# Chunked attention and a Mish feed-forward: the scores of the third group of heads follow the values directly, and sums of w_out's units 5 to 7 move

## The chip, the core and the metric

One core of a Trainium2 chip runs the whole program. The metric is the device time of one execution in microseconds (us). Engines: PE (TensorE, matmuls), PEld (its weight loads), DVE (VectorE), ACT (ScalarE), POOL (GpSimd), SP (the engine on whose queue nearly all transfers are issued).

## What is computed

The reference, cut down: attention inside chunks of 64 tokens, then a feed-forward layer with Mish, all in float32.

```python
scores = scale * np.matmul(q_c, k_c.transpose(0, 1, 2, 4, 3))
scores = scores - np.max(scores, axis=-1, keepdims=True)
attn = np.exp(scores)
attn = attn / (np.sum(attn, axis=-1, keepdims=True) + 1e-09)
out = np.matmul(attn, v_c)
...
h = x @ w_in
sp = np.where(h > 20.0, h, np.log1p(np.exp(np.minimum(h, 20.0))))
g = h * np.tanh(sp)
return (g @ w_out).astype(np.float32)
```

x is the attention's output, 4608 tokens of 512 values; w_in is 512 x 2048, w_out 2048 x 512.

## The kernel before

**Blocks.** The tokens are cut into 18 pairs of 256. A first block does pairs 0 and 1; then blocks m = 1 to 4 do four pairs each. While block m multiplies, the attention of the four pairs of block m + 1 is done beside it, so m = 4 has none. Every float32 operand is split into a rounded upper part and a rest, and a product is three sets of matmuls. Both layers use Strassen-like seven-product schemes, so sums of weight quarters are needed as operands: they are made on the chip once, stored to device memory, and loaded again as `w`/`late` tiles by `load_op` (line 831), nine products ahead of their use.

**Blocks m = 2 to 4** (BOTH_FROM = 2, line 797) have an upward half, `up_two(m, n)` for n = 0 to 3 (line 1087), and a downward half, `down_all(m)`. One `up_two` works on two units of w_in, i = 0 and 1, and runs the seven products k = 0 to 6 for each of them in turn. A product is six matmuls of 128x512. After product k of unit i the program calls `beside(h)` with h = 2k + i, so h counts 0 to 13, and all other work is hung on h. The engines take their instructions strictly in the written order (`manual_schedule`).

**Evictions in up_two** (lines 1150 to 1182). PSUM banks x (two of tag h), y and v (o0 to o3, given out by `flip`) hold the sums. x is copied by ACT after k = 0, 2 and 4 (G11, G21, G22; lines 1155, 1160, 1162) and read by Mish after k = 5 (G12). y is added by DVE to G11 after k = 1. v is added to G22 after k = 4 and to G21 after k = 6 (line 862). Mish activations (line 540) follow each. So the next product into a bank waits until that bank has been read.

**Attention beside it.** Pair j = first_pair(m + 1) + n belongs to n. Steps: `a_scores` (64x64 matmuls, line 298), `a_max` (324), `a_sub` (336), `a_exp` (345, ACT, with its own activation table, so that a table load stands before exp and before the next Mish), `a_inverse` (391 to 393), `a_norm` (398), `a_transpose` (409), `a_copy` (419, ACT), `a_values` (298), `a_raw` (430). From block GROUP_FROM on, the scores of pair j + 1 are done at h = 12 right behind the values of pair j, by `scores_apart` into the two y banks (line 359), with `max_apart` (370) at h = 12 and `sub_apart` (381) at h = 13; exp, inverse and normalisation then stand at h = 0, 2 and 3 of the next n. Before the change this holds for m = 3 alone; in m = 2 each n has its own scores at h = 1, and the steps at h = 1 to 7.

**Sums of w_out.** Unit u = 0 to 7 of w_out needs four steps: `t_whole` (line 237, DVE, adds upper part and rest), `t_sums` (246, DVE, three subtractions), `t_hi` (250, ACT cast to the upper part), `t_lo` (254, DVE, the rest) with the store of 1 MB to device memory on SP's queue (257). Units 4 to 7 are done in the upward half of m = 2 by the plan BUILDS_UP (line 888), which gives each step a place (n, h). Their tile is

```python
bld["o", u] = c_p.tile([P, 4, 2, 256], F32, name=f"t_{u}", tag="c")
```

and pool c_p has one buffer. In `beside` the order within one h is: S sums (`s_sums`: sums of two activated tiles of an earlier unit, lines 1078 and 1082), then the plan's steps, then attention. S sums in m = 2 stand at h = 5 and 9 of n = 1 to 3, two units' worth per n.

Of the kernel before, what the change touches and what calls it, by code (L numbers as in the profile page):

```python
# [24 lines left out]
def kernel(  # L25
# [244 lines left out]
    def load_qk(j, qk=None, ts=(BOTH,), queues=(nc.sync, nc.sync), pool=(at, "A")):  # L270
        if qk is None:
            if pool[0] is xo_p:
                both = xo_p.tile([P, 2, 2, H, CHUNK], F32, name=f"qk_{j}", tag="x")
                qk = [both[:, 0], both[:, 1]]
            else:
                qk = [
                    pool[0].tile([P, 2, H, CHUNK], F32, name=f"{n}_{j}", tag=pool[1]) for n in "qk"
                ]
        for t in ts:
            for x, src, queue in zip(qk, (q, k), queues):  # L280
                queue.dma_start(
                    out=x[:, t], in_=src[2 * j : 2 * j + 2][t].rearrange("t p h c -> p t h c")
                )
        st[j] = {"q": qk[0], "k": qk[1]}

    def load_v(j, vs=None):
        if vs is None:
            vs = at.tile([P, 2, H, D], F32, name=f"v_{j}", tag="A")
        nc.sync.dma_start(out=vs, in_=v[2 * j : 2 * j + 2].rearrange("t p h c -> p t h c"))
        st[j]["v"] = vs  # L290
# [23 lines left out]
    def a_scores(j, t=BOTH, place=HOME):  # L314
        small_mm(banks(j, "s", t, place), st[j]["q"], st[j]["k"], t)
# [7 lines left out]
    def a_max(j, t=BOTH):  # L323
        nc.vector.tensor_reduce(
            out=small(j, "m", t),
            in_=st[j]["s", t.start].rearrange("p c t g k -> p c (t g) k"),
            op=ALU.max,
            axis=AX.X,
        )

    def a_sub(j, t=BOTH):
        d = st[j]
        if t.start == 0:
            d["p"] = at.tile([P, 2, NG, 2, CHUNK], F32, name=f"p_{j}", tag="A")
        m = d["m", t.start]
        nc.vector.tensor_tensor(
            out=d["p"][:, t].rearrange("p t g c k -> p c (t g) k"),
            in0=d["s", t.start].rearrange("p c t g k -> p c (t g) k"),
            in1=m.unsqueeze(3).broadcast_to([P, 2, m.shape[2], CHUNK]),
            op=ALU.subtract,  # L340
        )

    def a_exp(j, t=BOTH):
        p = st[j]["p"][:, t]
        nc.scalar.activation(out=p, in_=p, func=AF.Exp, scale=SCALE)
# [42 lines left out]
    def a_inverse(j, t=BOTH):  # L388
        p = st[j]["p"][:, t].rearrange("p t g c k -> p (t g) c k")
        r = small(j, "r", t)  # L390
        nc.vector.tensor_reduce(out=r.rearrange("p c n -> p n c"), in_=p, op=ALU.add, axis=AX.X)
        nc.vector.tensor_scalar(out=r, in0=r, scalar1=1e-9, scalar2=None, op0=ALU.add)
        nc.vector.reciprocal(out=r, in_=r)

    def a_norm(j, t=BOTH):
        p = st[j]["p"][:, t].rearrange("p t g c k -> p c (t g) k")
        r = st[j]["r", t.start]
        nc.vector.tensor_tensor(
            out=p, in0=p, in1=r.unsqueeze(3).broadcast_to([P, 2, r.shape[2], CHUNK]), op=ALU.mult
        )  # L400
# [14 lines left out]
    def a_copy(j, t=BOTH):  # L415
        d = st[j]
        if t.start == 0:
            d["ps"] = at.tile([P, 2, H, CHUNK], F32, name=f"ps_{j}", tag="A")
        nc.scalar.copy(
            out=d["ps"][:, t].rearrange("p t h k -> p (t h k)"),  # L420
            in_=d["pt", t.start][:, : t.stop - t.start].rearrange("p t g n -> p (t g n)"),
        )
# [39 lines left out]
    def first_pair(m):  # L462
        return PAIRS + 4 * (m - 1)
# [159 lines left out]
    def run(plan_, key):  # L623
        for step, arg in plan_.get(key, ()):
            step(arg)
# [169 lines left out]

    LOOK, MORE = 5, 4
    BOTH_FROM = 2
    GROUP_FROM = BOTH_FROM + 1
    PRODUCTS = (
        ("A11", "B11"),  # L800
        ("A12", "B21"),
# [74 lines left out]
    def t_plan(*begins):  # L876
        plan_ = {}
        for n, places in begins:
            for step, place in zip(T_STEPS, places):
                plan_.setdefault(place, []).append((step, n))  # L880
        return plan_
# [4 lines left out]
    for n in range(NU):  # L886
        BUILDS_DOWN.setdefault(n + 1, []).append((t_keep, n))
    BUILDS_UP = t_plan(
        (4, [(0, h) for h in (4, 5, 6, 10)]),
        (5, [(0, 13), (1, 0), (1, 1), (1, 4)]),  # L890
        (6, [(1, h) for h in (10, 11, 12, 13)]),
        (7, [(2, h) for h in (4, 10, 12, 13)]),
    )

    def unit(m, u):
# [178 lines left out]
    def flip(m):  # L1074
        return OPEN if (m - BOTH_FROM) % 2 == 0 else (OPEN[0], OPEN[2], OPEN[1])
# [8 lines left out]
    def s_sums(u):  # L1084
        s_one(u)
        s_three(u)

    def up_two(m, n):
        units = (2 * n, 2 * n + 1)
        xt, yt, vt = flip(m)  # L1090
        j = first_pair(m + 1) + n
        on = m < QUADS
        x, y, v_ = {}, {}, {}

        def beside(h):
            at_ = (5, 9) if m == BOTH_FROM else (1, 2)
            if h in at_ and n:
                s_sums(2 * n - 2 + at_.index(h))
            if m == BOTH_FROM:
                run(BUILDS_UP, (n, h))  # L1100
            if h in (10, 11) and n == NU // 2 - 1:
                ready.append(operand(0, h - 10))
            if not on:
                return


            ahead = n and m >= GROUP_FROM
            if h == 1:
                if not ahead:
                    a_scores(j)  # L1110
                if m >= GROUP_FROM and not n:
                    load_qk(j + 1, pool=(ob_p, "ob"))
                load_v(j)
            if h == 2 and not ahead:
                a_max(j)
            if h == 3:
                if not ahead:
                    a_sub(j)
                if n < 3 and (n or m < GROUP_FROM):
                    load_qk(j + 1, pool=(ob_p, "ob"))  # L1120
            if h == (0 if ahead else 4):
                a_exp(j)
            if h == (2 if ahead else 6):
                a_inverse(j)
            if h == (3 if ahead else 7):
                a_norm(j)
            if h == 10:
                a_transpose(j)
                a_copy(j)
            if h == 12 and n < 3:  # L1130
                a_values(j)
                if m < GROUP_FROM:
                    a_raw(j)
                else:
                    scores_apart(j + 1, yt)
                    a_raw(j)
                    max_apart(j + 1)
            if h == 13 and n < 3 and m >= GROUP_FROM:
                sub_apart(j + 1)

        for k in range(7):
            for i, u in enumerate(units):
                if k == 0:
                    x[u] = bank(f"x_{m}_{u}", xt[i])
                    for name in GS:
                        z_new(u, name)
                if k == 1:
                    y[u] = bank(f"y_{m}_{u}", yt[i])
                if k == 3:
                    v_[u] = bank(f"v_{m}_{u}", vt[i])  # L1150
                o = y[u] if k == 1 else v_[u] if k in (3, 6) else x[u]
                product(k, o, k in (0, 1, 3))
                z = {name: G[u, name] for name in ("G11", "G12", "G21", "G22")}
                if k == 0:
                    nc.scalar.copy(out=z["G11"], in_=o)
                elif k == 1:
                    add(o, z["G11"])
                    mish(z["G11"], z["G11"])
                elif k == 2:
                    nc.scalar.copy(out=z["G21"], in_=o)  # L1160
                elif k == 4:
                    nc.scalar.copy(out=z["G22"], in_=o)  # L1162
                    add(v_[u], z["G22"])
                    if i:
                        for u_ in units:
                            mish(G[u_, "G22"], G[u_, "G22"])
                elif k == 5:
                    mish(z["G12"], o)
                elif k == 6:
                    add(o, z["G21"])  # L1170
                    mish(z["G21"], z["G21"])
                beside(2 * k + i)

    ready = []
# [5 lines left out]
    def operand(k, u):  # L1180
        d = {}
        g = G[u, TYPES[k][0]]
        d["gh"] = part("gh", f"gh_{k}_{u}")
        nc.scalar.copy(out=d["gh"], in_=g)  # L1184
        d["gl"] = part("gl", f"gl_{k}_{u}")
        parts["n"] += 1
        nc.vector.tensor_tensor(out=d["gl"], in0=g, in1=d["gh"].bitcast(F32), op=ALU.subtract)  # L1187
        return d
# [239 lines left out]
```

## Time and profile before

| | us |
|---|---|
| median of 3 runs (lowest to highest) | 806.84 (806.28 to 808.19) |
| the profiled execution's own time | 804.22 |
| its span, first to last instruction | 802.4 |
| PE busy | 787.6 (98%) |
| PEld busy | 680.7 (85%) |
| DVE busy | 547.5 (68%) |
| ACT busy | 462.6 (58%) |
| mean DMA traffic | 244 GB/s |

An engine's busy time is the time in which one of its instructions runs. PE's matmuls are pipelined and their ends are modelled, so PE's 98% does not mean that it is at its peak. The chain of waits follows the work that ended last back to the beginning; a piece of it ends when the next begins. In a list of instructions in order of time, the bracket at the end of a line tells how long the engine had been idle before it and what released it.

### The profile page before, as it was taken

What the parts mean: (1) busy time and instruction counts of PE and PEld (TensorE: products, weight loads), DVE (VectorE), ACT (ScalarE), POOL (GpSimd) and SP (SyncE); (2) the same over time, 40 slices, a digit from 0 to 9 for tenths busy, and PEclk for the clock granted to TensorE, in tenths of its full rate; (3) what the DMA queues carried; (4) which work ended last, traced back from release to release, by engine and by line L of the source; (5) the groups of instructions that cost most, each with busy time, mean ns of one, the idle gap of its engine ahead of it and who ended that gap; (6) DMA issues with size and microseconds to landing.
All of it is one profiled execution on the core that took longest, in us unless ns stands there. A gap on an engine that the chain in (4) does not pass through costs nothing.

```text
span 802.4 us, 16472 instructions
## 1 busy us (share of the span) xinstructions
PE 787.6 (98%) x6394; PEld 680.7 (85%) x6394; DVE 547.5 (68%) x835; ACT 462.6 (58%) x694; POOL 0.7 (0%) x6
## 2 busy tenths in 40 slices
PE   4999999999999999999999999999999999999998
PEld 4888787788888888888999998888999988888887
DVE  6789898655656786676688945545698723338875
ACT  5998976534436445566655737566556434455443
POOL 0000000000000000000000000000000000000000
PEclk9999999999999999999999999999999999999999
DMA  9999989877685879988667797776676776766774
GB/s 339 310 327 346 344 290 303 296 229 275 199 296 165 292 249 284 344 297 268 180 179 214 208 279 241 246 253 199 173 209 184 235 219 194 193 195 187 214 193 130
DMA packets 101581, 196.12 MB, mean 244 GB/s; under 512 B 10112, under 2 KB 26496, under 8 KB 99456
## 3 DMA queue, kind: packets, MB, share of 16 engines
q1 hardware_dynamic: 100896, 194.29, 76.2%
q8 instruction: 51, 0.84, 0.4%
q10 hardware_dynamic: 608, 0.79, 0.3%
q14 instruction: 26, 0.21, 0.1%
HBM read 152.04 MB, written 42.99 MB: 243 GB/s over the span
## 4 chain that ended last, share of the span: by engine, by line
PE 96%; DVE 1%; DMA 1%; ACT 1%; issue 0%; ACTq 0%; DVEq 0%
PE x L850 22%; PE X L1279 12%; PE v L850 11%; PE Z L1279 6%; PE y L850 6%; PE o L565 6%; PE h L527 5%; PE Y L1279 3%; PE X_a L1231 3%; PE X L1231 3%; PE Z L1231 3%; PE av L298 2%; PE s L298 2%; PE pt L409 2%; PE Y L1231 1%; PE o_(1, 1)_0_2789 L565 1%
## 5 line engine op out<-in xcount | busy, mean ns | idle before, releaser
L1184 ACT CAST gh<-g 128x512 fp32r<-128x512 f32 x168 | 103.5, 621 | 93.1 <-PE X L1279 29.9
L1187 DVE TENSOR_TENSOR gl<-g,gh 128x512 fp32r<-128x512 f32 x168 | 115.2, 689 | 49.0 <-ACT gh L1184 45.3
L850 PE MATMUL x<-x_T,w 128*128 128x512 f32 x390 | 97.3, 391 | 0.0
L850 PEld LDWEIGHTS x<-x_T,w 128*128 128x128 f32 x390 | 72.6, 188 | 15.4 <-ACT zb L964 0.4
L862 DVE TENSOR_TENSOR g<-v,g 128x512 f32<-128x512 f32 x48 | 33.0, 690 | 73.2 <-ACT g L1162 41.9
L540 ACT ACTIVATE g<-g 128x512 f32<-128x512 f32 x72 | 44.9, 631 | 59.2 <-DVE g L862 58.9
L527 PE MATMUL h<-x_first,wi 128*128 128x512 f32 (+1 forms) x216 | 47.4, 371 | 1.1 <-ACT x_first L449 0.7
L850 PE MATMUL x<-x_T,late 128*128 128x512 f32 x186 | 46.0, 391 | 0.0
L527 PEld LDWEIGHTS h<-x_first,wi 128*128 128x128 f32 x216 | 36.8, 188 | 8.2 <-ACT x_first L449 0.8
L850 PEld LDWEIGHTS x<-x_T,late 128*128 128x128 f32 x186 | 34.6, 188 | 7.0
L1279 PE MATMUL X<-w,gh 128*128 128x256 f32 x288 | 40.5, 283 | 0.0
L565 PE MATMUL o<-wo,gh 128*128 128x512 f32 x128 | 39.5, 390 | 0.0
L1279 PEld LDWEIGHTS X<-w,gh 128*128 128x128 f32 x288 | 37.2, 192 | 0.1
L862 DVE TENSOR_TENSOR g<-y,g 128x512 f32<-128x512 f32 x24 | 16.3, 680 | 30.2 <-PE y L850 29.6
L1162 ACT COPY g<-x 128x512 f32<-128x512 f32 x24 | 14.1, 589 | 37.2 <-PE x L850 37.2
L850 PE MATMUL v<-x_B,w 128*128 128x512 f32 x138 | 35.3, 395 | 0.1
L850 PE MATMUL y<-x_B,w 128*128 128x512 f32 x126 | 31.8, 395 | 0.0
L850 PE MATMUL x<-x_B,w 128*128 128x512 f32 x126 | 31.6, 393 | 0.0
L1279 PE MATMUL X<-late,gh 128*128 128x256 f32 x224 | 31.5, 283 | 0.0
L850 PEld LDWEIGHTS v<-x_B,w 128*128 128x128 f32 x138 | 25.4, 188 | 6.2 <-DVE zb L862 1.0
L850 PE MATMUL v<-x_T,w 128*128 128x512 f32 x120 | 29.6, 390 | 0.0
L1279 PEld LDWEIGHTS X<-late,gh 128*128 128x128 f32 x224 | 28.9, 192 | 0.1
(217 smaller groups left out, 1736.0 us busy)
## 6 DMA issues: line engine op xcount, KB each, us to landing
w<-wa SPq DMA_DIRECT2D x150, 256.0 KB, 3.8
w<-wb SPq DMA_DIRECT2D x94, 256.0 KB, 2.9
late<-wa SPq DMA_DIRECT2D x74, 256.0 KB, 3.1
late<-wb SPq DMA_DIRECT2D x74, 256.0 KB, 2.9
wst<-in_w_in SPq DMA_DIRECT2D x16, 512.0 KB, 5.7
wst<-in_w_out SPq DMA_DIRECT2D x16, 512.0 KB, 6.0
v<-in_v SPq DMA_DIRECT2D x16, 512.0 KB, 6.4
wa<-a SPq DMA_DIRECT2D x6, 1024.0 KB, 4.4
```

Source lines behind the costliest of these rows:

```text
L298: nc.tensor.matmul(o[h * CHUNK : (h + 1) * CHUNK, c, t - ts.start, g], lhsT=l[rows, t, 2 * g + h], rhs=r[rows, t, 2 * g + h], start=True, ...
L409: nc.tensor.transpose(out=d["pt", ts.start][:, t - ts.start, g], in_=d["p"][:, t, g].rearrange("p c k -> p (c k)"), identity=ident,)
L527: nc.tensor.matmul(h[:, cols], lhsT=wi[i // 2][:, i % 2 * 2 + kt // 2, w_, kt % 2], rhs=x[:, x_, kt, cols], start=(n == 0), stop=(n == 3 * ...
L540: nc.scalar.activation(out=out_, in_=in_, func=AF.Mish)
L565: nc.tensor.matmul(acc[t], lhsT=g[:, t * P : (t + 1) * P], rhs=wo[f // 2][:, f % 2, part], start=(f == 0 and n == 0), stop=(f == NF - 1 an ...
L850: nc.tensor.matmul(o, lhsT=t[:, w_, kt], rhs=x[x_][:, kt], start=(start and i == 0), stop=(i == 5), skip_group_check=not start,)
L862: nc.vector.tensor_tensor(out=z, in0=o, in1=z, op=ALU.add)
L1162: nc.scalar.copy(out=z["G22"], in_=o)
L1184: nc.scalar.copy(out=d["gh"], in_=g)
L1187: nc.vector.tensor_tensor(out=d["gl"], in0=g, in1=d["gh"].bitcast(F32), op=ALU.subtract)
L1231: nc.tensor.matmul(o, lhsT=d[g][:, t * P : (t + 1) * P], rhs=w__, start=(first and n == 2), stop=(u == NU - 1 and g == "gl"), skip_group_c ...
L1279: nc.tensor.matmul(o, lhsT=d[g][:, t * P : (t + 1) * P], rhs=w_[:, part], start=(k in (0, 1, 3) and u == 0 and t % 2 == 0 and n == 0), sto ...
```

## The change

It does three things in block m = 2. GROUP_FROM falls from 3 to 2, so that block 2 takes block 3's order: scores of pair j + 1 behind the values of pair j for n = 0 to 2, the following steps at their earlier places, and q and k of the second pair loaded at h = 1 of n = 0 instead of h = 3. The plan BUILDS_UP gets new places: unit 4's `t_lo` from h = 10 to h = 7; unit 5 from (0, 13), (1, 0), (1, 1), (1, 4) to (0, 11), (0, 12), (0, 13), (1, 4); unit 6 from h = 10 to 13 to h = 7, 8, 10, 11 of n = 1; unit 7 from h = 4, 10, 12, 13 to h = 4, 8, 10, 11 of n = 2. And the second S sums of each n move from h = 9 to h = 6.

```diff
     BOTH_FROM = 2
-    GROUP_FROM = BOTH_FROM + 1
+    GROUP_FROM = BOTH_FROM
...
     BUILDS_UP = t_plan(
-        (4, [(0, h) for h in (4, 5, 6, 10)]),
-        (5, [(0, 13), (1, 0), (1, 1), (1, 4)]),
-        (6, [(1, h) for h in (10, 11, 12, 13)]),
-        (7, [(2, h) for h in (4, 10, 12, 13)]),
+        (4, [(0, h) for h in (4, 5, 6, 7)]),
+        (5, [(0, 11), (0, 12), (0, 13), (1, 4)]),
+        (6, [(1, h) for h in (7, 8, 10, 11)]),
+        (7, [(2, h) for h in (4, 8, 10, 11)]),
     )
...
         def beside(h):
-            at_ = (5, 9) if m == BOTH_FROM else (1, 2)
+            at_ = (5, 6) if m == BOTH_FROM else (1, 2)
             if h in at_ and n:
                 s_sums(2 * n - 2 + at_.index(h))
```

## Rows read from the trace of the kernel before

**Rows 1.** The page: the chain that ended last, by engine.

```profile
PE 96%; DVE 1%; DMA 1%; ACT 1%; issue 0%; ACTq 0%; DVEq 0%
```

**Rows 2.** Stretches: length, busy us of PE, PEld, DVE, ACT, POOL; granted clock, DMA share, GB/s.

```profile
303.00:325.00 22.00, 22.00 (x219) 18.00 (x219) 12.82 (x17) 13.65 (x19) 0.00 (x0) 1.00 0.99 325
...
10.00:12.00 2.00, 1.22 (x5) 0.85 (x5) 2.00 (x4) 1.02 (x3) 0.00 (x0) 1.00 1.05 386
```

**Rows 3.** The chain in order of time: start, us; ends of both upward halves.

```profile
302.97 2.72 PE x L850 x12
...
391.95 2.87 PE X L1279 x24
...
473.86 2.75 PE x L850 x12
...
561.70 2.87 PE X L1279 x24
```

**Rows 4.** PE in order of time: start, us; m = 2 first, then m = 3.

```profile
319.10 1.03 PE L409 MATMUL pt<-ident,p 128*128 128x128 f32 x8
...
322.80 1.16 PE L298 MATMUL av<-ps,v 64*64 64x64 f32 x64
...
493.71 1.16 PE L298 MATMUL av<-ps,v 64*64 64x64 f32 x64
...
499.95 2.88 PE L850 MATMUL y<-x_B,w 128*128 128x512 f32 x12
...
514.44 1.52 PE L850 MATMUL v<-x_B,w 128*128 128x512 f32 x6
515.90 1.16 PE L298 MATMUL av<-ps,v 64*64 64x64 f32 x64
```

**Rows 5.** DVE in order of time: m = 2 first, then m = 3.

```profile
313.20 1.61 DVE L246 TENSOR_TENSOR t<-t 128x512 f32<-128x512 f32 x3
314.73 1.21 DVE L391 TENSOR_REDUCE r<-p 128x16 f32<-128x1024 f32 x1
...
316.47 1.22 DVE L398 TENSOR_TENSOR p<-p,r 128x1024 f32<-128x1024 f32 x1
317.61 0.68 DVE L862 TENSOR_TENSOR g<-v,g 128x512 f32<-128x512 f32 x1
...
328.43 1.23 DVE L237 TENSOR_TENSOR t<-wo 128x1024 f32<-128x1024 f32 x1 [2.15 <-DMA wb<-t]
...
495.86 1.29 DVE L370 TENSOR_REDUCE m<-s 128x8 f32<-128x512 f32 x2 [1.35 <-PE s L359]
...
498.04 1.28 DVE L381 TENSOR_TENSOR p<-s,m 128x512 f32<-128x512 f32 x2
```

**Rows 6.** ACT in order of time: m = 2 first, then m = 3.

```profile
314.89 1.05 ACT L250 CAST t<-t 128x1024 fp32r<-128x1024 f32 x1
...
319.83 1.15 ACT L540 ACTIVATE g<-g 128x512 f32<-128x512 f32 x2
...
499.40 1.28 ACT L345 ACT_TABLE_LOAD   x1
500.69 1.06 ACT L345 ACTIVATE p<-p 128x1024 f32<-128x1024 f32 x1
...
513.39 1.01 ACT L419 COPY ps<-pt 128x1024 f32<-128x1024 f32 x1
```

**Rows 7.** Landing: stores of units 4 to 7; unit 4's alone; w loads issued 318 to 320.

```profile
DMA to landing us min/median/max: 5.0/5.7/7.9
...
DMA to landing us min/median/max: 7.9/7.9/7.9
...
w<-wa SPq DMA_DIRECT2D x2, 256.0 KB, 6.9
```

**Rows 8.** PE in order of time, early in the span.

```profile
10.78 1.08 PE L409 MATMUL pt<-ident,p 128*128 128x128 f32 x4 [3.06 <-DVE p L398]
...
20.29 0.60 PE L409 MATMUL pt<-ident,p 128*128 128x128 f32 x4
```

## The prediction

> **What bounds the kernel now.** The page's chain of waits comes first: the work that ended last is TensorE's for 96% of the span [rows 1]. The stretch table then shows the third group's scores at full load: TensorE is busy for all 22.00 us of 303 to 325 at a granted clock of 1.00 [rows 2]. So here a change gains only what it takes off TensorE, and costs whatever wait it puts in front of TensorE; VectorE and ScalarE count only where TensorE has to wait for a bank or an operand of theirs.
>
> Two stretches of the chain are twins. The upward half of m = 2 runs from 302.97 to 391.95, 88.98 us; that of m = 3, which already has the order the change extends, from 473.86 to 561.70, 87.84 us [rows 3]. Neither has a wait of TensorE in it. The twin differs in one thing that matters below: it has no sums of w_out beside it.
>
> **Part 1, values and scores together.** m = 2 becomes like m = 3 on TensorE: three scores (of n = 1, 2, 3) follow the values before them, so three switches into and out of 64-wide matmuls go. The price is the difference of the twins, 88.98 - 87.84 = 1.14 us, or 0.38 each. This is all that can be gained, as no wait stands in the stretch to be removed. The chip does the same matmuls. The q and k of the next pair are asked for two places earlier, and are needed at h = 12, behind the values that start at 322.80 [rows 4], instead of h = 1 of the next n. They are asked for once the first two products are done, at 302.97 + 2.72 = 305.7; with the 9.2 us worked out below as the longest landing there are 7.9 us to spare for SP's queue: nothing. Exp moves to h = 0 between two evictions with two table loads per n as in the twin, and the S sums from h = 9 to h = 6 in VectorE's free time: nothing by themselves.
>
> **Part 2, unit 4's rest and store three places earlier.** At h = 7 the subtraction t_lo(4) takes the place of the normalisation, which began at 316.47 [rows 5]; its cast had ended at 314.89 + 1.05 = 315.94 [rows 6], so it waits for nothing. Instructions in a row start 1.14 apart when they last 1.22 (316.47 to 317.61), 0.08 less than their length; I use this for all. The normalisation then ends at 316.47 + 1.14 + 1.22 = 318.83, the transposes start at 319.10 [rows 4]: covered, with 0.27 to spare. The two adds behind it end by 320.05, before the second activation of the pair at 319.83 [rows 6] asks. The store of 1 MB leaves at 317.7 instead of 320.4.
>
> **Part 3, unit 5: the single buffer.** All of t(4) to t(7) live in one buffer of pool c, so t_whole(5) may write only when the store of t(4) has landed. The trace shows that wait: at 328.43 VectorE had been idle 2.15 us for the store [rows 5], 7.9 us after its issue [rows 7]. That wait was free, since VectorE had no urgent work. Now t_whole(5) stands at h = 11. The landing is the unknown: the four stores took 5.0 to 7.9 [rows 7]. I take 7.9, the same store in the same stretch, as a quarter-size load there already took 6.9 [rows 7]. The upper end is that load plus 0.75 MB at the stretch's 325 GB/s [rows 2], 6.9 + 2.3 = 9.2. So t_whole(5) starts at 317.7 + 7.9 = 325.6.
>
> Behind it on VectorE queue the add of G21, t_sums(5), the two maxima, the second add and the two subtractions that empty the score banks: 325.6 + 1.15 + 0.61 + 1.53 + 1.21 + 0.61 + 0.68 = 331.4 for the first subtraction [rows 5]. Those banks are the next y banks. TensorE wants y at 322.80 + (499.95 - 493.71) = 329.04 [rows 4]. **Stall: 2.35 us** (0 if the store lands in 5.0; 3.65 if in 9.2).
>
> ScalarE is late with it. The second add ends at 330.8, then come an activation (0.58, half of the pair's 1.15), the cast of unit 5 (1.05), a copy (about as long as an activation), a table load (1.28), exp (1.06) and the second copy of x [rows 6]: 335.9. TensorE, from 331.4 with 1.36 per product (2.72 for 12 matmuls [rows 3]), wants that x at 335.5. **Stall: 0.4 us.**
>
> **Part 4, unit 6.** In n = 1 the exp ends at 335.3. Then 1.74 for the inverse (314.73 to 316.47 [rows 5]), 0.61 for an add, 1.14 for the normalisation and 1.22 for t_lo(5): the store leaves at 340.0. t_whole(6) now stands at h = 7, with only four S sums (0.69 each, as the add) between: VectorE is there at 342.7, 2.7 us after the issue, and no store lands in that. I take 5.0, the shortest [rows 7], because SP stands still in front of this store and the loads ahead of it are few; the other end is 7.9. So t_whole(6) starts at 345.0.
>
> Behind it: the add of the first G22 ends at 345.0 + 1.15 + 0.69 = 346.85; TensorE wants to go on with v at 331.4 + 0.4 + (514.44 - 499.95) = 346.3 [rows 4]. **Stall: 0.55 us.** t_sums(6) comes before the second add, which ends at 346.76 + 1.53 + 0.69 = 349.0. On ScalarE its activation, G12's (0.58 each), then the cast of unit 6 (1.05), which the code issues ahead of the copy of the transposed p (1.01 [rows 6]): 352.2. The values want that copy at 346.85 + (515.90 - 514.44) = 348.3 [rows 4]. **Stall: 3.9 us**, the largest.
>
> SP's own queue: the store waits from h = 4 to 340.0 with the loads of later products behind it. Those are nine products ahead, and n = 2 cannot begin before the values of 352.2; issued at 340 and landing even 9.2 later they are in time: nothing.
>
> **Part 5, unit 7.** t_lo(6) lies seven places ahead of t_whole(7), so no wait for the store. t_sums(7) and the cast (1.53 + 1.05) come ahead of the copy of p, which in the twin ends at 513.39 + 1.01 = 514.40 [rows 6] with the values at 515.90, 1.50 us of room: at most 1.1, at least 0; I take **0.3**, since VectorE has idle time in front of that second add.
>
> **Sum:** -1.14 + 2.35 + 0.4 + 0.55 + 3.9 + 0.3 = +6.4 us. The profiled execution would go from 804.22 to 810.6 (span 802.4 to 808.8). It lies 2.6 us below the median of the runs, 806.84, to which I add the same: **813.2 us**. Ends: with 5.0 for the first store and nothing but the 3.9 and 0.3 left, +3.1, or 809.9; with 9.2 and 7.9, +1.3 and +2.9, or 817.4. This kernel's measurement can tell about 0.2%, 1.6 us.
>
> **The clock, a row and a rule.** Early in the span TensorE was idle for 3.06 us and its next four transposes took 1.08 us, later 0.60 [rows 8], although the granted clock read 1.00, the 2.4 GHz level, there too [rows 2]. The Trainium skill, "TensorE: Matmul & The Clock Gate", section "Why this matters for your kernels", warns that a gap between bursts of matmuls drops the array from 2.4 to 1.2 GHz. By that rule the change would lose more than its waits; the trace's clock column does not show such a drop. The sum above keeps full speed; the slow transposes make it a rival.
>
> **Rivals.** (a) Not slower: the store does not hold the buffer long. Place: t_whole(5) and t_whole(6). It decides if the store in n = 1 lands within 2.7 us, and that in n = 0 by 323.2, within 5.5. Then the first three stalls are gone, and of the 3.9 between 0 and 2.1 stays, because the cast and t_sums still stand ahead of the copy of p: taken as 1.05, -1.14 + 1.05 + 0.3 = +0.2, 807.0 us; with nothing left of them the full gain, 805.7 us. Against it: 5.0 us is the shortest landing, and the row of the 2.15 us wait shows the hold. Both are within 0.2%; more than 1.6 us of gain has no source. (b) TensorE runs slower behind the wait of 3.9 us: at 1.08/0.60 = 1.8 times its time for, say, three products, 3 x 1.36 x 0.8 = 3.3 more: 816.5 us. For it speak the transposes, against it the clock column.
>
> **How the numbers follow.** Forecast 0.72, (b) 0.10, (a) 0.18. The first two are slower by over 0.2%: 0.82. Of (a), 0.15 is within 0.2% and 0.03 is left for a faster time from something I do not see. The range from 808.8 to 816.5 takes nearly all of the forecast's ends and most of (b), and leaves out (a).
>
> **What would show it.** In the profile after: VectorE idle in front of line 237 in n = 0 and n = 1 with the store as releaser; TensorE idle before y of n = 1 for VectorE, and before the values of n = 1 for ScalarE's copy (line 419), some 4 us; m = 2's upward half near 95 us instead of 88.98, all else unchanged. If t_whole(6) starts without a wait, or that half comes out under 89, I am wrong.

## The result and the profile after

The changed kernel takes 816.96 us (median of 4 runs, 816.29 to 817.83) against 807.52 us before; the ratio is 1.0115, 95% interval 1.009 to 1.014. The forecast was 813.2 us in a range from 808.8 to 816.5: the direction and the three places of the waits in n = 1 were right, the size was too small, and the median lies 0.5 us above the range.

The stretch that the change touches is the upward half of m = 2, from its first product to the first matmul of the downward half. In TensorE's list it ran from 302.81 to 391.78 before (88.97 us). After, the list in order of time (start, us, what, idle before and releaser):

```profile
306.77 2.88 PE L850 MATMUL x<-x_B,w 128*128 128x512 f32 x12
...
326.75 1.16 PE L298 MATMUL av<-ps,v 64*64 64x64 f32 x64
327.73 0.52 PE L359 MATMUL s<-late 64*64 64x64 f32 x23
330.10 0.81 PE L359 MATMUL s<-late 64*64 64x64 f32 x41 [1.84 <-issue]
...
335.78 2.99 PE L850 MATMUL y<-x_B,late 128*128 128x512 f32 x12 [0.55 <-PE x L850]
...
351.76 1.65 PE L850 MATMUL v<-x_B,late 128*128 128x512 f32 x6 [1.00 <-DVE g L862]
356.88 1.16 PE L298 MATMUL av<-ps,v 64*64 64x64 f32 x64 [3.46 <-ACT ps L419]
357.86 1.82 PE L359 MATMUL s<-late 64*64 64x64 f32 x64
359.61 2.48 PE L850 MATMUL v<-x_B,w 128*128 128x512 f32 x6
...
404.36 0.88 PE L1279 MATMUL X<-w,gh 128*128 128x256 f32 x6
```

The half is now 404.36 - 306.77 = 97.59 us, 8.62 longer, where [rows 3, 4] had no wait at all. TensorE waits before y, v and values of n = 1, as forecast, and once in the middle of the scores that stand in n = 0 (the 41 matmuls at 330.10; the releaser "issue" means that the trace shows none), which was not forecast. From the end of the half to the end of the span it is 410.7 us, as before (410.6). Ahead of the half the code is the same; its 306.77 against 302.81 is scatter between executions, as the runs below, from 303.8 to 308.0, show. So I compare halves, and the times of whole runs beside them. A half is read from the one profiled execution of a kernel.

VectorE's list of the same kernel has the reason. (The bracket before y names TensorE's own product before it. What y waits for is the bank that the first of the two subtractions at 334.99 empties: half of their 1.28 us later it is 335.6, and y starts at 335.78.)

```profile
329.94 1.23 DVE L237 TENSOR_TENSOR t<-wo 128x1024 f32<-128x1024 f32 x1 [6.13 <-DMA wb<-t]
...
333.20 1.28 DVE L370 TENSOR_REDUCE m<-s 128x8 f32<-128x512 f32 x2
334.40 0.68 DVE L862 TENSOR_TENSOR g<-v,g 128x512 f32<-128x512 f32 x1
334.99 1.28 DVE L381 TENSOR_TENSOR p<-s,m 128x512 f32<-128x512 f32 x2
...
349.88 1.23 DVE L237 TENSOR_TENSOR t<-wo 128x1024 f32<-128x1024 f32 x1 [3.13 <-DMA wb<-t]
...
353.15 0.68 DVE L862 TENSOR_TENSOR g<-v,g 128x512 f32<-128x512 f32 x1
```

Both t_whole wait for the store of the unit before, 6.13 and 3.13 us, where [rows 5] had one wait of 2.15 that nobody behind it felt. The stores of units 4 and 5, from the list of issues (KB, us to landing), answer to [rows 7]:

```profile
wb<-t SPq DMA_DIRECT2D x1, 1024.0 KB, 8.3
...
wb<-t SPq DMA_DIRECT2D x1, 1024.0 KB, 5.7
```

ScalarE's list shows the cast of unit 6 ahead of the copy of p that the values wait for:

```profile
354.88 1.03 ACT L250 CAST t<-t 128x1024 fp32r<-128x1024 f32 x1
355.81 1.01 ACT L419 COPY ps<-pt 128x1024 f32<-128x1024 f32 x1
```

And the table of stretches (length, busy times, then granted clock, DMA share, GB/s) shows the clock:

```profile
357.00:358.00 1.00, 1.00 (x76) 1.00 (x80) 0.77 (x2) 0.52 (x2) 0.00 (x0) 1.00 0.00 0
358.00:361.40 3.40, 3.40 (x72) 2.98 (x64) 1.29 (x2) 1.33 (x2) 0.00 (x0) 0.50 1.00 338
361.40:365.00 3.60, 3.60 (x17) 2.91 (x16) 1.89 (x3) 2.10 (x3) 0.00 (x0) 1.00 0.55 141
```

Behind the wait of 3.46 us the granted clock was 0.50, the 1.2 GHz level, until 361.4.

Each loss is the time between two starts less the time between the same two starts in the twin, m = 3 of the kernel before (for the values 5.12 us from 351.76 to 356.88, less 515.90 - 514.44 = 1.46 [rows 4]):

| lost against the twin, us | forecast | after |
|---|---|---|
| values of n = 0 to y of n = 1 | 2.35 | 2.79 |
| second copy of x, n = 1 | 0.4 | 0.33 |
| v of n = 1 | 0.55 | 1.17 |
| values of n = 1 | 3.9 | 3.66 |
| scores and v at the lower clock | 0 (a rival: 3.3) | 1.52 |
| values of n = 2 | 0.3 | 0.26 |
| sum, and less the 1.14 gained | 7.5, +6.4 | 9.7, +8.6 |

The +8.6 lies within the interval of the timed difference (0.9% to 1.4% of 807.5 is 7.3 to 11.3 us).

### The profile page after: what moved, and what is told of

Its sections match the earlier page's. It is cut to its first block, busy times and chain, and to the rows that moved or that the text cites. A ratio compares the mean times of both kernels' runs of the same rounds, so it can differ in the third digit from the quotient of the medians.

```text
span 815.1 us, 16477 instructions
## 1 busy us (share of the span) xinstructions
PE 793.6 (97%) x6394; PEld 684.1 (84%) x6394; DVE 547.3 (67%) x841; ACT 462.9 (57%) x694; POOL 0.7 (0%) x6
## 4 chain that ended last, share of the span: by engine, by line
PE 82%; DMA 7%; DVE 6%; ACT 3%; issue 1%; SPq 1%; ACTq 0%; DVEq 0%
PE x L850 17%; PE X L1279 11%; PE v L850 9%; PE Z L1279 6%; PE y L850 4%; PE h L527 4%; PE Y L1279 3%; PE X_a L1231 3%; PE X L1231 3%; PE Z L1231 3%; PE o L565 2%; PE av L298 2%; DMA wb<-t 2%; PE pt L409 1%; PE Y L1231 1%; PE o_(1, 1)_0_2789 L565 1%
```

## The experiments

Halves are measured as above, each in one execution; with no wait left a half would be 87.84, as the twin. That execution was the slowest of ten timed in run 3, and the fastest of twelve in runs 4 and 9. Ratios are to the kernel before. In the runs with added lines, line numbers are 2 or 8 higher.

| run | upward half of m = 2, us | ratio and interval |
|---|---|---|
| before | 88.97 | 1 |
| after | 97.59 | 1.0115 (1.009 to 1.014) |
| 1 order alone | 91.40 | 1.0004 (0.999 to 1.0018) |
| 2 places alone | 97.26 | one execution |
| 3 second buffer | 92.11 | 1.0025 (1.0013 to 1.0038) |
| 4 second buffer, cast behind | 89.11 | 1.0015 (0.9998 to 1.0031) |
| 5 unit 6 back | 92.04 | one execution |
| 6 unit 5 back | 95.18 | one execution |
| 7 busy wait | 96.42 | one execution |
| 8, 16 matmuls more | 89.00 | 0.9996 (0.9979 to 1.0013) |
| 8, 92 matmuls more | 90.92 | one execution |
| 9, 16 more, q and k at h = 3 | 87.82 | 0.9994 (0.9978 to 1.001) |

**1. The order alone.** The kernel before with nothing but the new order, q and k at h = 1 included: BUILDS_UP and the S sums keep their old places.

```diff
-    GROUP_FROM = BOTH_FROM + 1
+    GROUP_FROM = BOTH_FROM
```

> Only the order of the third group is changed; the sums of w_out and the S sums keep the places they had before. My theory (one buffer for the sums, held until the store has landed): t_whole(5) at (0, 13) waits for a store that leaves at about 320.4 and lands some 8 us later, and now it stands ahead of the subtraction that empties the score banks, so TensorE waits 1.2 to 1.6 us before y of n = 1, and nowhere else. That gives back the 1.14 us of the order: an upward half of m = 2 of about 89.2 us, no measurable difference to the kernel before (ratio 0.999 to 1.001). Rival (the new order itself costs time in m = 2): the half is 92 us or more and the ratio above 1.003.

The half was 91.40, not about 89.2. The timed runs show no measurable difference, but the place was not the one named. Of the 3.56 us lost against the twin, 2.28 stand in the scores of n = 0 and 0.99 in those of n = 1, with no engine as releaser; t_whole(5) found its store landed. Neither theory had this.

```profile
326.36 0.52 PE L359 MATMUL s<-late 64*64 64x64 f32 x23
328.93 0.82 PE L359 MATMUL s<-late 64*64 64x64 f32 x41 [2.05 <-issue]
```

**2. The places alone.**

```diff
-    GROUP_FROM = BOTH_FROM
+    GROUP_FROM = BOTH_FROM + 1
```

> Only the new places of the sums and S sums; the third group keeps its old order. My theory: the places are the harm, with either order. t_whole(5) waits at (0, 11) without delaying TensorE there, because no scores need emptying; t_whole(6) at (1, 7) waits for the store of unit 5 and stands in front of the normalisation, so TensorE waits about 3 us before the transposes of n = 1 and about 2 more before the values: an upward half of 94 to 96.5 us against 88.98. Rival (only both together do harm, through the score banks): below 91 us.

The half was 97.26, 0.8 above the upper end: the places do the harm by themselves. VectorE's two waits are there with the old order, and TensorE's behind them, at the transposes and the values of n = 1:

```profile
331.51 1.23 DVE L237 TENSOR_TENSOR t<-wo 128x1024 f32<-128x1024 f32 x1 [6.43 <-DMA wb<-t]
...
349.05 1.23 DVE L237 TENSOR_TENSOR t<-wo 128x1024 f32<-128x1024 f32 x1 [2.28 <-DMA wb<-t]
```

```profile
334.95 1.16 PE L298 MATMUL s<-late 64*64 64x64 f32 x64 [1.45 <-ACT raw L430]
...
351.56 1.06 PE L409 MATMUL pt<-ident,p 128*128 128x128 f32 x8 [2.98 <-DVE p L398]
...
357.19 1.16 PE L298 MATMUL av<-ps,v 64*64 64x64 f32 x64 [1.80 <-ACT ps L419]
...
381.46 1.16 PE L298 MATMUL av<-ps,v 64*64 64x64 f32 x64 [1.62 <-ACT ps L419]
```

Two waits more had not been counted: 1.45 us of the scores of n = 1 for the raw copy of n = 0 (they share banks in the old order), and 1.62 us of the values of n = 2 for the copy of p.

**3. A second buffer.**

```diff
+        elif u == 5:
+            bld["o", u] = wo_p.tile([P, 4, 2, 256], F32, name="t_5", tag="o4")
         elif u != 3:
             bld["o", u] = c_p.tile([P, 4, 2, 256], F32, name=f"t_{u}", tag="c")
```

> The whole change, but the tile of unit 5 lies in the place of w_out's unit 4, which is free once t_whole(4) has read it, so neither t_whole(5) nor t_whole(6) has a store in front of it. My theory: VectorE's two waits (6.13 and 3.13 us) go, and with them TensorE's waits before y and v, most of that before the values and the fall of the clock. What is left is the cast and t_sums in front of the copy of p in n = 1 and n = 2, 1.0 to 1.6 us together: an upward half of 89.0 to 89.6 us instead of 97.6, ratio to the kernel before 0.998 to 1.002. Rival (the sums stand in front of evictions and delay them wherever their buffer lies): the half stays above 95 us.

Both waits of VectorE for a store are gone, and TensorE's before y and v with them; the clock stays at 1.00. The values of n = 1 wait 0.74 us for the copy behind the cast. So the store was the cause of these. But the half is 92.11, not 89.0 to 89.6, and 2.8 us of what is lost stand again in the scores of n = 0:

```profile
327.11 0.52 PE L361 MATMUL s<-late 64*64 64x64 f32 x23
330.21 0.81 PE L361 MATMUL s<-late 64*64 64x64 f32 x41 [2.58 <-issue]
...
351.93 1.16 PE L300 MATMUL av<-ps,v 64*64 64x64 f32 x64 [0.74 <-ACT ps L421]
```

**4. Second buffer, and the cast behind the copy of p.**

```diff
-        (6, [(1, h) for h in (7, 8, 10, 11)]),
-        (7, [(2, h) for h in (4, 8, 10, 11)]),
+        (6, [(1, h) for h in (7, 9, 11, 12)]),
+        (7, [(2, h) for h in (4, 9, 11, 12)]),
```

> As the run with the second buffer, and for units 6 and 7 t_sums stands at h = 9 instead of 8, the cast at h = 11 instead of 10, behind the copy of p, and the rest at h = 12. My theory: nothing is left that TensorE waits for, the full gain of 1.14 us comes through: an upward half of 87.8 to 88.1 us, ratio to the kernel before 0.9975 to 0.9995. Rival (the copy of p is late for another reason): the wait before the values of n = 1 stays at 1 us.

The waits for the copy of p are gone from n = 1 and n = 2. The half is 89.11, not 87.8 to 88.1: all of the 1.3 us that remain stand in the scores, 0.87 in n = 0, again behind 23 matmuls, and 0.43 in n = 1. The ratio, 1.0015, is above the expected 0.9975 to 0.9995 too. In three kernels with quite different timing (runs 1, 3 and 4) the wait stands in front of the same matmul.

```profile
326.97 0.81 PE L361 MATMUL s<-late 64*64 64x64 f32 x41 [0.65 <-issue]
```

**5 and 6. One unit back at a time.** Unit 6 (first line) or unit 5 (second) at its old places.

```diff
-        (6, [(1, h) for h in (7, 8, 10, 11)]),
+        (6, [(1, h) for h in (10, 11, 12, 13)]),
...
-        (5, [(0, 11), (0, 12), (0, 13), (1, 4)]),
+        (5, [(0, 13), (1, 0), (1, 1), (1, 4)]),
```

> The changed kernel with unit 6's four steps back at h = 10 to 13 of n = 1. My theory: the two waits for a store are separate costs. What is lost before y of n = 1 stays (about 3.5 to 4 us against the twin, block 3), the waits before v and the values of n = 1 go, and with them the clock's fall (granted clock 1.00 all through): an upward half of 92 to 93.5 us instead of 97.59. Rival (one delay of VectorE's queue from n = 0 on drags through n = 1, whatever unit 6 does): the waits in n = 1 stay and the half is 95 us or more.

> The changed kernel with unit 5's steps back at (0, 13), (1, 0), (1, 1) and (1, 4). My theory: t_whole(6) at (1, 7) still waits for the store of unit 5, and the values of n = 1 for the copy of p, 3 to 4 us, with or without a fall of the clock behind it; in n = 0 about 2.3 us are lost as in the run with the order alone. An upward half of 94 to 97 us. Rival (the delay of n = 0 is what makes n = 1 late): below 93 us.

The halves were 92.04 and 95.18, both where expected. With unit 6 back TensorE waits in n = 0 (3.4 us lost up to the second copy of x), not before v or values of n = 1, and the clock stays at 1.00. With unit 5 back t_whole(6) waits 3.52 us for its store, v waits 0.77 and the values 3.46, and the clock falls to 0.50 from 353.1 to 356.5. The two waits are separate costs. In n = 0 of the second run the loss was another than expected: 0.83 us before x at h = 11, whose weights landed late; see 8 and 9.

With unit 6 back:

```profile
328.99 0.81 PE L359 MATMUL s<-late 64*64 64x64 f32 x41 [0.84 <-issue]
...
335.91 3.00 PE L850 MATMUL y<-x_B,late 128*128 128x512 f32 x12 [1.77 <-issue]
```

With unit 5 back:

```profile
323.31 1.63 PE L850 MATMUL x<-x_T,w 128*128 128x512 f32 x6 [0.59 <-DMA w<-wa]
...
353.15 1.99 PE L298 MATMUL av<-ps,v 64*64 64x64 f32 x64 [3.46 <-ACT ps L419]
```

**7. The wait filled with work.**

```diff
             if h == 12 and n < 3:
+                if n == 1 and m == BOTH_FROM:
+                    o = bank("unread_2", yt[0])
+                    for _ in range(32):
+                        nc.tensor.matmul(
+                            o[:, 0:PTOK], lhsT=ones[:, 0:P], rhs=ones, start=True, stop=True
+                        )
                 a_values(j)
```

> The changed kernel with 32 more matmuls of 128x256 on a bank that nobody reads, ahead of the values of n = 1, some 3.5 us of work in the place of TensorE's wait there. My theory (the clock fell to 0.5 from 358.0 to 361.4 because TensorE had been idle): the granted clock stays 1.00, scores and v behind the wait take 1.1 and 1.6 us again instead of 1.8 and 2.5, and the upward half is 1.0 to 1.6 us shorter than 97.59, with more work in it. Rival (the slow matmuls have another cause, such as transfers): scores and v stay slow, and the half is as long or longer.

```profile
351.64 3.67 PE L1134 MATMUL unread<-ones 128*128 128x256 bf16 x32
355.26 1.16 PE L298 MATMUL av<-ps,v 64*64 64x64 f32 x64
356.24 1.11 PE L359 MATMUL s<-late 64*64 64x64 f32 x64
357.29 1.66 PE L850 MATMUL v<-x_B,w 128*128 128x512 f32 x6
```

The values still come when the copy is there, and scores and v take 1.11 and 1.66 us instead of 1.82 and 2.48. The stretches of this run say why, and that the clock can fall elsewhere:

```profile
329.00:333.00 4.00, 4.00 (x12) 3.13 (x11) 3.93 (x8) 1.54 (x2) 0.00 (x0) 0.57 0.31 78
355.00:360.00 5.00, 5.00 (x143) 4.24 (x142) 3.46 (x6) 2.53 (x5) 0.00 (x0) 1.00 0.74 252
```

The half is 1.17 us shorter with more work in it. In this run the clock fell at 329.3 instead, behind a wait of 1.70 us in the scores of n = 0; in run 3 the same wait was 2.58 us and the clock stayed at 1.00, as it did behind the 2.98 us before the transposes in run 2. So a gap's length alone does not tell whether it falls. Behind the unfilled wait of 3.46 us it fell in both kernels that have it, the changed one and run 6; that the filling kept it up here rests on one execution, in which it had already fallen once.

**8. The seam of instructions.** The kernel of run 4 with 16 small matmuls early in the span, and with 92.

```diff
         nc.tensor.matmul(o[:, 0:PTOK], lhsT=ones[:, 0:P], rhs=ones, start=True, stop=True)
+        if "more" not in idle:
+            idle["more"] = True
+            for _ in range(16):
+                nc.tensor.matmul(
+                    o[:, 0:CHUNK], lhsT=ones[:, 0:P], rhs=ones[:, 0:CHUNK], start=True, stop=True
+                )
```

> As the run with the second buffer and the cast behind, and 16 small matmuls (32 instructions of TensorE) on an unread bank in an idle time of TensorE near 8 us. What is left there is a wait of TensorE that no other engine ends, always in front of the 24th matmul of a chunk column's scores, instruction 5569 of its records (and 6081 = 5569 + 512). My theory: TensorE's instructions come in pieces of 256 by transfers on queue 8 (51 of 16 KB); values and scores directly behind each other use one piece up in 2 us, and the next is late where the transfers are busy. 32 more instructions before move the seam 16 matmuls ahead, to the 8th scores matmul, and give the piece 2.7 us more time: the wait in n = 0 is there or gone, at most 0.3 us, and the half is 87.8 to 88.5 us instead of 89.11; ratio to the kernel before 0.9965 to 1.001. Rival (that matmul waits for its data, or the scores bank): the wait stays in front of the 24th matmul, 0.6 us or more.

> As the run with 16 extra matmuls, but 92 (184 instructions of TensorE). My theory (pieces of 256 instructions): the seam that stood in front of the 24th scores matmul of n = 0 now falls just ahead of the values, and the next one 256 instructions on, in front of the 61st scores matmul, give or take one; the piece behind it is asked for only some 6 us before, in the stretch where transfers are slowest, so a wait of 1 to 5 us stands there: an upward half of 89 to 93 us. The time before m = 2 may grow by a few us and is not compared. Rival (the matmul waits for its data or its bank): a wait of about 0.6 us in front of the 24th, none at the 61st.

The theory is that a seam between two pieces of 256 instructions stands in front of that matmul. A matmul here is two instructions, its weight load and itself, so 256 instructions are 128 matmuls. With 92 more matmuls ahead, the seam must fall at 23 - 92 + 128 = 59 matmuls into the scores. The trace of that run:

```profile
329.14 1.09 PE L361 MATMUL s<-late 64*64 64x64 f32 x59
332.03 0.34 PE L361 MATMUL s<-late 64*64 64x64 f32 x5 [1.79 <-issue]
```

The wait moved exactly there; it does not belong to the data of that matmul. With 16 more it is gone from n = 0 and n = 1. The page's line for queue 8 fits in number: TensorE's 6394 matmuls and as many weight loads, 12,788 instructions, in 51 pieces are about 250 each, and 0.84 MB are about 66 bytes for one (the engine's few other instructions are not counted):

```profile
q8 instruction: 51, 0.84, 0.4%
```

Between 318 and 331 in the changed kernel one such transfer is recorded, starting at 327.6; TensorE went on at 330.10, 2.5 us later. In all seven kernels that stop in n = 0, TensorE went on 2.3 to 2.6 us after the start of such a transfer. In run 6, which has the same order and no stop there, it started at 319.7, 7.8 us before the 24th matmul. That ties the stop to this transfer.

The Trainium skill, "Runtime: NRT & Kernel Launch", section "Instruction fetch mechanics", says that instructions are refilled in blocks of 16 KiB, 256 instructions, and that crossing a block is mostly hidden. The size agrees with the runs; the cost, up to 2.58 us in run 3, does not.

With 16 more matmuls the half was still 89.00, not at most 88.5: a wait of another kind, in n = 0 at h = 11 (1.18 us lost), for weights that were asked for at 315.1 and took 8.9 us to land:

```profile
324.17 1.63 PE L858 MATMUL x<-x_T,w 128*128 128x512 f32 x6 [0.94 <-ACT g L542]
...
w<-wa SPq DMA_DIRECT2D x1, 256.0 KB, 8.9
```

The releaser named here is ScalarE, but the load landed at 324.0, just before x began; in run 6 the trace names the load itself for the same wait.

**9. q and k where they were.**

```diff
-                if m >= GROUP_FROM and not n:
+                if m > BOTH_FROM and not n:
                     load_qk(j + 1, pool=(ob_p, "ob"))
...
-                if n < 3 and (n or m < GROUP_FROM):
+                if n < 3 and (n or m == BOTH_FROM):
```

> As the run with 16 extra matmuls, but q and k of the second pair are asked for at h = 3 of n = 0 in m = 2, as in the kernel before. There x of n = 0 at h = 11 waited 0.94 us, and w loads issued ahead of it took 8.3 to 8.9 us. My theory (1 MB of q and k ahead of the weights on SP's queue makes those weights late): the wait goes, nothing is left that TensorE waits for, and the half is 87.8 to 88.2 us; the whole 1.14 us is there, ratio to the kernel before 0.9965 to 1.000. Rival (the weights are late through the store of unit 4 or the queue's general load): 0.5 us or more of that wait stays, 88.5 us or more; or q and k come late for the scores at h = 12.

```profile
303.79 2.88 PE L858 MATMUL x<-x_B,w 128*128 128x512 f32 x12
...
324.76 1.11 PE L361 MATMUL s<-late 64*64 64x64 f32 x64
...
391.61 1.11 PE L1287 MATMUL X<-w,gh 128*128 128x256 f32 x8
...
w<-wa SPq DMA_DIRECT2D x1, 256.0 KB, 6.6
```

No wait is left: 391.61 - 303.79 = 87.82 us, the twin's length. The weights for the same x were asked for at 311.3, ahead of q and k, and took 6.6 us. One execution without this wait would prove little, since only three of the nine kernels with q and k ahead of that load show it. The landing does more. In the twin this x begins 17.1 us into the half; measured against that time the load came between 0.8 us early and 1.0 us late in those nine, and with q and k behind it 3.4 us (the kernel before) and 3.0 us (this run) early.

The half of this kernel has the change's whole gain, 1.15 us against before, and by the two ratios it is 1.2% faster than the changed kernel; against the kernel before the timed runs cannot show a gain of that size (0.9994, interval 0.9978 to 1.001), nor tell it from the run with 16 matmuls (0.9996).

## Why the prediction was wrong in size

**Right.** Part 1's price: 1.14 us, which the half of run 9 gives back whole. Part 2: free. Parts 3 to 5, the mechanism: the single buffer holds both t_whole, and the cast stands ahead of the copy of p. Runs 2, 3, 5 and 6 show it: the second buffer takes the waits away, each unit's move takes away its own. The largest term, 3.9 us, measured 3.66. Rival (a) is out: the stores took 8.3 and 5.7 us, not 5.5 and 2.7.

**The step that failed** is the clock: "The sum above keeps full speed; the slow transposes make it a rival." By the forecast's own sum TensorE would be idle for 3.9 us, and the sum went on at full speed behind it. The clock fell to 0.50 and cost 1.52 us; run 7 ties that to the idle time. Against the rival I had set a granted clock of 1.00 early in the span, where transposes took 1.08 us; that entry was no evidence, since the clock's records of that execution begin only at 14.9 us. In the run with 16 matmuls they begin at 8.3 us, and there the same four transposes took 0.63 us while the clock was 1.00, and the next four 1.12 us while it was 0.50:

```profile
10.52 0.63 PE L411 MATMUL pt<-ident,p 128*128 128x128 f32 x4 [2.20 <-DVE p L400]
...
13.40 1.12 PE L411 MATMUL pt<-ident,p 128*128 128x128 f32 x4
...
11.70:15.10 3.40, 3.13 (x54) 2.16 (x46) 3.26 (x7) 1.57 (x4) 0.00 (x0) 0.50 1.00 377
```

So the slow transposes of [rows 8] were most likely the lower clock itself, and no row stood against the rival. The Trainium skill, "TensorE: Matmul & The Clock Gate", section "Why this matters for your kernels", warns of gaps between bursts of matmuls, and the trace here agrees with it: 0.50 behind the gap of 3.46 us. The rival's own price, 3.3 us, was more than twice what was lost: the clock was low only from 358.0 to 361.4, not for three products at 1.8 times their length. That its 816.5 us lies near the measured 816.96 is luck, as the terms below had to make up the rest.

**Mis-sized terms.** The store of unit 5 was taken at 5.0 us, "because SP stands still in front of this store and the loads ahead of it are few"; it took 5.7, and the wait before v was 1.17 us instead of 0.55. The store of unit 4, 8.3 instead of 7.9, added 0.4. These and the clock come to 2.6 us; the other terms came out 0.4 smaller, which leaves the 2.2 us by which the half was longer than forecast. Of the 3.8 us between 813.2 and 816.96, 0.7 more is the kernel before itself, whose median with a fourth run came to 807.52 instead of 806.84; the remaining 0.9 is not located and lies within the scatter of whole runs.

**Not seen, though it cost nothing in the changed kernel itself.** The wait for instructions in the scores was hidden there: VectorE was still waiting for the store, and took up the scores 2.3 us after their end at 330.9. Run 5 shows it too: the stop was 0.84 us instead of 1.84, and TensorE stood 1.77 instead of 0.55 before y. Once the store's waits are gone, the stop and the weights behind q and k take all of the gain in the half (run 4, and the run with 16 matmuls). On q and k the prediction said "nothing", having asked only whether they come in time, not what they delay on SP's queue.

## What to carry to other kernels

Before moving a step earlier, look for the buffer that it writes: if that is the only one, its last reader, a store included, moves onto the path of everything queued behind the step. A wait of a few us in the bounding engine can have a lower clock behind it, as in three of these kernels (behind 1.70 and twice 3.46 us), and the price of that, here 1.5 us, belongs in the range. And a stretch dense in small matmuls can run out of instructions: where an engine stops in the middle of a group with no releaser, add a few instructions ahead and see whether the stop moves. And a load put earlier on a queue is to be asked for what stands behind it there, not only whether it comes in time.

## What the runs showed that was not expected

TensorE's instructions arrive in transfers of 16 KB, 256 instructions each (run 8). Values and scores behind each other use 256 in 2 us, and in six kernels TensorE then stood still for 0.65 to 2.58 us in front of the same instruction, until 2.3 to 2.6 us after such a transfer had started. Why the transfer starts late is open. That the DMA engines are busy there is an inference: block 3 of the kernel before has the same sequence at 285 GB/s and shows no stop, against 392 GB/s from 318 to 331 in the changed kernel, though where its seams fall was not followed up. But runs 6 and 9 show no stop in n = 0 either, with 402 and 399 GB/s in 13 us around the same place. So the traffic alone does not decide it, and it was not varied by itself.
